# Issuing the five engine programs straight into the main block of a fused attention and GLU kernel

## Chip, cores and metric

One core of one Trainium2 chip. The metric is the device time of one execution in microseconds (us). The *span* is the time from the first to the last instruction record of an execution; it is shorter than the device time. The three sets of experiments ran on three different chips, so times are compared within a set.

## The reference, cut

```python
def _A_ref(x, wqkv, wo):            # sliding window attention: 32 heads of 18, window 256
    ...
def _B_ref(x, w_gate, w_up, w_down):
    g = jnp.einsum("bsd,df->bsf", x, w_gate)
    u = jnp.einsum("bsd,df->bsf", x, w_up)
    h = _sigmoid(g) * u
    return jnp.einsum("bsf,fd->bsd", h, w_down)

x = A_x                              # 2048 x 576, bf16
xn = _layernorm(x, axis=-1)
s = _A_ref(xn, A_wqkv, A_wo)
g = _silu(_B_ref(xn, B_w_gate, B_w_up, B_w_down))   # hidden size 4608
return x + s * g
```

## The kernel before

The kernel builds a graph of operations, orders it with its own scheduler, and then emits one program for each engine. Only the emission matters here. `run_engine` writes an engine's instructions with their semaphore waits. Ahead of SyncE's last operation, which is the last store of the output, it writes a wait for every DMA lane (semaphore) that is not an output lane; after it, a wait for the output lanes.

```python
        def run_engine(e, eng):
            known = {}
            for o in self.prog[e]:
                if e == "SP" and o is self.prog[e][-1]:
                    for i, n in enumerate(lane_cnt):
                        if n > 0 and i not in outs:
                            eng.wait_ge(lanes[i], n)        # housekeeping waits
                # ... the operation's own waits, the operation, its semaphore update ...
            if e == "SP":
                for i in outs:
                    eng.wait_ge(lanes[i], lane_cnt[i])      # the output has landed
                eng.nop()

        with nc.Block() as block:
            @block.tensor
            def _(eng):
                run_engine("PE", eng)
            # ... scalar, vector, gpsimd and sync likewise ...
```

`nc.Block()` gives each engine a block of its own with a branch into it and a branch out of it, and closes with an all-engine barrier: each engine drains and signals, GpSimd gathers the signals and releases the others.

The softmax here doesn't subtract the row's maximum and nothing guards it: scores larger than these inputs give would overflow.

## Time and profile before

| | before |
|---|---|
| device time, median of the first 3 runs | 560.82 us (560.54 to 561.11) |
| span of the profiled run, its device time | 558.90 us, 560.63 us |
| TensorE busy | 553.0 us, 99% of the span |
| last store lands (SyncE's wait ends) to end of the span | 0.437 us |

The prediction below shows the lines. Two habits help. In the source view of a line, each row is one engine's instructions of that line: durations in ns, then the first and the last start in us. A "q" after an engine's name marks its sequencer, which waits, branches and issues and never counts as busy. Where a start or end is quoted to the nanosecond, it is from the trace's records.

### The profile page before, as it was taken

The page shows a single profiled execution, that of the slowest core. Times are in us where ns is not written, and L with a number is a line of the kernel's source. Part 1 is how long each engine was busy: PE and PEld are TensorE (multiplying, and loading weights), DVE is VectorE, ACT ScalarE, POOL GpSimd, SP SyncE. Part 2 cuts the span into 40 slices and gives each one's busy share as a digit, 9 for nine tenths or more (in the row PEclk, how much of TensorE's full clock was granted, in tenths as well). Part 3 has the DMA queues.
Part 4 walks back from the last instruction along what each step waited for, and adds up shares of the span by engine and source line. Part 5 has one row for each costly group of instructions (what it writes and reads, how often), then busy time and mean ns, then how long its engine had stood idle before and what let it go on. Part 6 is the DMA issues. An engine that isn't in the chain of part 4 may idle for free.

```text
span 558.9 us, 19273 instructions
## 1 busy us (share of the span) xinstructions
PE 553.0 (99%) x8342; PEld 339.5 (61%) x8342; DVE 333.6 (60%) x797; ACT 274.3 (49%) x383; POOL 210.8 (38%) x360
## 2 busy tenths in 40 slices
PE   8999999999999999999999999999999999999996
PEld 7454444677755545467886555545688754444786
DVE  5477788687568767574558757357567623333033
ACT  4245654443657655645656464565756342323011
POOL 5564456566245444440667534035373200000000
PEclk9999999999999999999999999999999999999999
DMA  8988997831125534435121264244501035551010
GB/s 224 311 239 191 218 270 221 204 51 45 54 71 155 161 110 144 139 112 95 28 62 44 78 196 115 84 134 130 166 24 47 20 110 154 160 171 48 2 45 23
DMA packets 113468, 67.83 MB, mean 121 GB/s; under 512 B 18620, under 2 KB 111516, under 8 KB 113384
## 3 DMA queue, kind: packets, MB, share of 16 engines
q1 hardware_dynamic: 105960, 60.68, 39.8%
q0 software_dynamic: 7424, 5.92, 4.0%
q8 instruction: 66, 1.08, 0.8%
q14 instruction: 18, 0.15, 0.1%
HBM read 55.15 MB, written 2.36 MB: 103 GB/s over the span
## 4 chain that ended last, share of the span: by engine, by line
PE 98%; DVE 1%; DMA 0%; issue 0%; DVEq 0%
PE ps L121 94%; PE ps L800 3%; DMA x<-in_A_x_dram 0%; DVE small L524 0%; DVE small L526 0%; PE ps L598 0%; DVE xnr L540 0%; DVE s_attn L1061 0%; DVE thf L1066 0%; DVE xnr L544 0%; DVE small L528 0%; DVE small L530 0%; DVE xf L1071 0%; DVEq L1226 0%
## 5 line engine op out<-in xcount | busy, mean ns | idle before, releaser
L121 PE MATMUL ps<-xnT,wgs 64*128 64x512 bf16 (+1 forms) x2400 | 282.5, 368 | 0.1
L750 ACT ACTIVATE expr<-ps 128x1024 bf16<-128x1024 f32 (+4 forms) x160 | 154.9, 969 | 77.8 <-PE ps L121 77.2
L121 PEld LDWEIGHTS ps<-xnT,wgs 64*128 64x128 bf16 x2400 | 113.9, 94 | 114.8 <-DVE hT L948 1.6
L121 PE MATMUL ps<-wd_sb,hT 64*128 64x288 bf16 (+2 forms) x2448 | 156.7, 276 | 0.0
L948 DVE SCALAR_TENSOR_TENSOR hT<-tring,ps 128x512 bf16<-128x512 bf16 x144 | 98.3, 683 | 94.5 <-ACT tring L945 93.4
L945 ACT ACTIVATE tring<-ps 128x512 bf16<-128x512 f32 x144 | 86.1, 598 | 129.7 <-PE ps L121 127.5
L121 PEld LDWEIGHTS ps<-wd_sb,hT 64*128 64x128 bf16 x2448 | 112.4, 94 | 28.6
L278 POOL DMA_DIRECT2D qk<-qd x160 | 82.5, 522 | 119.4 <-PE ps L121 109.5
L763 DVE TENSOR_TENSOR expr<-expr,mask 128x128 bf16<-128x128 bf16 (+2 forms) x240 | 63.6, 298 | 62.0 <-ACT expr L750 61.5
L714 POOL TENSOR_SCALAR kx<-kprev,small 128x256 bf16<-128x256 bf16 x64 | 61.4, 969 | 28.1 <-PE ps L121 27.4
L121 PE MATMUL ps<-qk,kx 64*128 64x320 bf16 (+1 forms) x704 | 59.4, 254 | 0.0
L278 POOL DMA_DIRECT2D oT<-o2T x72 | 36.5, 514 | 58.5 <-DVE o2T L826 49.6
L121 PE MATMUL ps<-xnT,wgr 64*128 64x512 bf16 (+1 forms) x300 | 55.9, 367 | 0.0
L121 PEld LDWEIGHTS ps<-qk,kx 64*128 64x128 bf16 x704 | 31.2, 94 | 21.5 <-ACT expr L750 0.5
L121 PE MATMUL ps<-xnT,wqk 64*128 64x512 bf16 x256 | 32.6, 376 | 0.0
L1051 ACT ACTIVATE thf<-ps 128x576 bf16<-128x576 f32 (+3 forms) x22 | 11.4, 519 | 39.7 <-PE ps L121 39.4
L818 DVE STREAM_TRANSPOSE ot<-ps 128x512 f32<-128x512 f32 x32 | 22.4, 700 | 11.6 <-PE ps L800 11.5
L714 DVE TENSOR_SCALAR kx<-qk,small 128x512 bf16<-128x512 bf16 x64 | 22.4, 378 | 4.7 <-PE ps L121 4.1
L121 PEld LDWEIGHTS ps<-xnT,wgr 64*128 64x128 bf16 x300 | 14.9, 94 | 16.5
L826 DVE STREAM_TRANSPOSE o2T<-o 128x512 bf16<-128x512 bf16 x32 | 22.7, 711 | 1.0
L636 DVE CAST qd<-ps 128x1024 bf16<-128x1024 f32 (+1 forms) x20 | 22.1, 1110 | 1.5 <-PE ps L121 1.5
L696 ACT ACTIVATE v_aug<-ps 64x288 bf16<-64x288 f32 x32 | 13.1, 409 | 17.3 <-PE ps L121 16.8
(71 smaller groups left out, 302.1 us busy)
## 6 DMA issues: line engine op xcount, KB each, us to landing
wgs<-in_B_w_gate_dram SPq DMA_DIRECT2D x72, 256.0 KB, 3.3
wgs<-in_B_w_up_dram SPq DMA_DIRECT2D x72, 256.0 KB, 3.7
wd_sb<-in_B_w_down_dram SPq DMA_DIRECT2D x9, 576.0 KB, 6.3
qk<-qd POOLq DMA_DIRECT2D x100, 36.0 KB, 2.7
wgr<-in_B_w_gate_dram SPq DMA_DIRECT2D x36, 64.0 KB, 2.2
wgr<-in_B_w_up_dram SPq DMA_DIRECT2D x36, 64.0 KB, 2.5
xf<-in_A_x_dram SPq DMA_DIRECT2D x16, 144.0 KB, 2.6
out_dram<-xf SPq DMA_DIRECT2D x15, 144.0 KB, 1.8
```

The source lines that it names most:

```text
L121: res = eng.matmul(outs[i], lhs(ROWS[t], i), rhs(ROWS[t], i), start=start, stop=stop, tile_position=(64 * t, 0))
L278: o = self.op(eng, DMA_ISSUE_NS[eng], lambda e: e.dma_start(dst, src), name, deps, prio, nbytes=nbytes)
L636: return eng.tensor_copy(dst, self.both(h, n))
L696: return eng.activation(dst, src, ACTF.Copy)
L714: return e.tensor_scalar(self.kx[:, sx, pos:pos + n_ // SW, t, :], src.rearrange("p (s k) -> p s k", k=SW), self.half[:, t:t + 1], None, A ...
L750: return eng.activation(self.expr[:, se, :, lo * SW:NT], self.both(h, NT)[:, :, lo * SW:NT], ACTF.Exp, scale=SM_SCALE)
L763: return eng.tensor_tensor(e_, e_, m_, ALU.mult)
L800: res = eng.matmul(outs[i][p0:p0 + VH, cols], self.v_aug[ROWS[i], o:o + VH], self.expr[ROWS[i], se, t, cols], start=n == 0, stop=n == len( ...
L818: return e.transpose(self.ot1[:, p1, :], self.halves(hp, NT)[i])
L826: t2 = op("DVE", dve_ns(NT), lambda e, p2=p2, p3=p3: e.transpose(self.o2T[:, p3, :], self.o2[:, p2, :]), f"ot2:{c}:{pr}:{i}", deps=[on, d3 ...
L945: th = op("ACT", act_ns(NT), lambda e: e.activation(self.tring[:, st, :], bank(h, 0), ACTF.Tanh, scale=0.5), f"th:{c}:{ft}", deps=[pg, dt_ ...
L948: mu = op("DVE", dve_ns(NT), lambda e: e.scalar_tensor_tensor(self.hT[:, ft, :], self.tring[:, st, :], 1.0, bank(h, 1), ALU.add, ALU.mult) ...
```

## The change

The intent is to do without the blocks: no branches, and no barrier at the end, since SyncE already waits for the output itself.

```diff
-        with nc.Block() as block:
-            @block.tensor
-            def _(eng):
-                run_engine("PE", eng)
-  ... (scalar, vector, gpsimd, sync likewise)
+        for e, eng in (("SP", nc.sync), ("POOL", nc.gpsimd), ("DVE", nc.vector), ("ACT", nc.scalar), ("PE", nc.tensor)):
+            run_engine(e, eng)
```

## The prediction

> **What bounds the kernel now.** I read the page's busy table and slices first, then the chain that ended last, then the two ends of the span, because the change touches nothing between them.
>
> ```profile
> span 558.9 us, 19273 instructions
> PE 553.0 (99%) x8342; PEld 339.5 (61%) x8342; DVE 333.6 (60%) x797; ACT 274.3 (49%) x383; POOL 210.8 (38%) x360
> PE   8999999999999999999999999999999999999996
> ...
> PE 98%; DVE 1%; DMA 0%; issue 0%; DVEq 0%
> ```
>
> The reader is to see that TensorE is busy in all slices but the first and the last, and that 98% of the chain is TensorE. Nothing in the middle can shrink unless matmuls go, and none do. A change to the frame round the program can act only in the first microsecond and in what follows the last matmul (the 6 in the last slice).
>
> The end, from the chain cut to 550 to 559 us:
>
> ```profile
> 549.98 4.54 PE ps L121 x170
> ...
> 554.92 0.28 DVE s_attn L1061
> ...
> 555.23 0.41 DVE thf L1066
> ...
> 555.66 0.27 DVE xf L1071
> ```
>
> TensorE ends at about 554.5, and VectorE finishes the last rows at 555.93. The span goes on for another 2.96 us, and that rest is SyncE's. The source views of the lines that SyncE runs last give it:
>
> ```profile
> L1216 SPq EVENT_SEMAPHORE  x31: 28/28/28, 554.9 to 556.8; - x31
> ...
> L1226 SPq EVENT_SEMAPHORE  x1: 28/28/28, 556.8 to 556.8; - x1
> ...
> L278 SPq DMA_DIRECT2D out_dram<-xf x1: 332/332/332, 556.9 to 556.9; - x1
> ...
> L1233 SPq EVENT_SEMAPHORE  x1: 1188/1188/1188, 557.3 to 557.3; - x1
> ```
>
> Columns are duration in ns (min, median, max), then first and last start. SyncE runs down 31 housekeeping waits at about 60 ns each, issues the last store at 556.89, and sits in its wait for that store until 558.458 (the trace's nanosecond record: 557.270 plus 1,188 ns). Only then comes what the change removes, on the line of the framework's block:
>
> ```profile
> L1235 POOLq EVENT_SEMAPHORE  x2: 17/17/17, 558.7 to 558.8; - x2
> L1235 POOLq DRAIN  x1: 10354/10354/10354, 446.2 to 446.2; - x1
> L1235 PEldq DRAIN  x1: 732/732/732, 553.8 to 553.8; - x1
> L1235 ACTq DRAIN  x1: 294/294/294, 554.9 to 554.9; - x1
> L1235 DVEq DRAIN  x1: 311/311/311, 555.7 to 555.7; - x1
> L1235 SPq COMPARE_BRANCH  x1: 41/41/41, 558.5 to 558.5; - x1
> L1235 SPq DRAIN  x1: 13/13/13, 558.7 to 558.7; - x1
> L1235 SPq EVENT_SEMAPHORE  x1: 17/17/17, 558.8 to 558.8; - x1
> L1235 ACTq EVENT_SEMAPHORE  x1: 17/17/17, 558.8 to 558.8; - x1
> L1235 DVEq EVENT_SEMAPHORE  x1: 21/21/21, 558.8 to 558.8; - x1
> L1235 PEldq EVENT_SEMAPHORE  x1: 51/51/51, 558.8 to 558.8; - x1
> ```
>
> The closing barrier is a drain per engine, a gather on POOL, and a release back to all. Four engines arrive early: their long drains (POOL's 10,354 ns) lie beside other work and cost nothing. SyncE arrives last, so only its branch, its drain, the gather and the release stand after the output.
>
> **What the Trainium skill says.** "Perfetto Trace Analysis", section "Sequencer-only Instruction (DRAIN, etc)": for such an instruction the profiler reports only the execution, not the semaphore wait or the propagation after it. The trace agrees: the records of the barrier after SyncE's branch have 13, 17, 17 and 51 ns on the path, while the time from that branch's end (558.537) to the last release record (558.895) is 358 ns; most of it is between records. So I take start-to-start distances, not durations. "VectorE: DVE Perf Modes", section "The DRAIN you can't avoid", puts frame drains at about 12 ns; SyncE's 13 agrees, the others are longer since their engines still had work. "Advanced Engine Details and Errata", section "Control Flow Timing", gives about 51 ns for an unconditional branch; the only branch recorded is SyncE's, 41 ns, followed by 138 ns to the next record. "Runtime: NRT & Kernel Launch", section "The ~15µs preamble/postamble breakdown", has the runtime's own barrier after the kernel, about 1.5 us; the trace holds no record of it, but the profiled execution's time, 560.63, is 1.73 us above its span of 558.90, so something of that size follows or precedes the span.
>
> **The change part by part.** The instruction orders of the two built programs differ only by the entry and exit branches of each engine, and the built program's last block, which the change drops, holds the barrier: four drains with their waits, and POOL's drain with its two semaphore instructions. Every matmul, DMA and wait keeps its place on its engine. The start-up barrier belongs to the framework's preamble, not to the block, and stays.
>
> At the end: after 558.458 the new SyncE program has one more wait (two output lanes, long since satisfied), where the old one has a wait folded into its branch. In the run of 31 waits one takes about 60 ns from end to end, so SyncE should end at 558.458 + 0.060 = 558.518. Before, the last record ends at 558.895. Saving: 0.377 us. It is wholly on the path, because nothing else is running.
>
> The parts of that 0.377: from the wait's end to SyncE's drain 0.217 (558.458 to 558.675), to POOL's gather 0.038 (558.713), to the release instruction 0.077 (558.790), to the latest engine's wake 0.054 (558.844), that record 0.051; sum 0.437, less the 0.060 that the remaining wait costs.
>
> At the start: five entry branches go. But none of them has a record, and SyncE's first DMA starts at 0.798, 66 ns after the start-up barrier released SyncE at 0.732. At the end, between its last wait (556.853) and the DMA (556.893), the gap is 40 ns with no branch at all. So an entry branch can have cost at most 26 ns, less than the exit branch with its 138 ns gap; I think the entries fall through. I count 0.013, half of it. VectorE's first memset begins 131 ns after its release, but the first matmuls it starts are warm-up, and the first real chain begins with the load of x, on SyncE.
>
> In the middle: 0. TensorE's order is unchanged.
>
> Sum inside the span: 0.377 + 0.013 = 0.39 us, so span 558.5 and time 560.82 - 0.39 = 560.43.
>
> Outside the span there are about 1.7 us that no record explains. With the barrier all five engines leave the program within some 60 ns of each other; without it four leave 2.5 us or more before SyncE, so whatever each one does before the runtime's own barrier is done by then. If SyncE is the slowest there too, this gains nothing; if another is, up to 1 us. My estimate, with no measurement behind the odds: 0.08 on average. The predicted time is 560.35.
>
> **The rivals.** One: the barrier was hidden, because the runtime's barrier replaces it and takes the same wait. Then the span shrinks by 0.39 but the time does not move: 560.8. For it: both gather on SyncE, and the output wait is the same. Against: the two stand in series, each with its own round of semaphores. Two: the early departure above frees a larger part of the 1.73 us, giving 559.5 to 560.0. For it: that part is four times larger than the removed barrier. Against: SyncE also has to pass through it, and it leaves last. Three: the code's place in memory moves by the few instructions dropped, so instruction fetches fall elsewhere. A stall on TensorE would add up to microseconds; but the chain now shows 0% "issue", over 8,342 matmuls, so the stream is fed with room to spare, and a straight stream is no harder to fetch than one with branches. I give it 0 to 0.1. Four: an engine that starts tens of nanoseconds earlier shifts the first transfers against each other; the start has slack in x's landing, and it would be worth 0.1 either way.
>
> **Range and chances.** The three runs before spread from 560.54 to 561.11, about 0.3 each way, as large as the effect. From the point 560.35, the second rival and a low draw give 559.8; the first rival with a little noise gives 560.9. Two per cent is 11.2 us, thirty times the barrier and more than everything outside TensorE's busy time (558.9 - 553.0 = 5.9). Faster by that needs something that the trace does not show: 0.01. Slower needs a fetch stall repeated through the program: 0.01.
>
> **What would show it.** Right: no record on the block's line at the end; the last record is SyncE's wait for the outputs, within 0.1 us after the last store lands; a span of 558.5; SyncE's first DMA still at 0.78 to 0.80; TensorE's busy time within 0.3 us of 553.0; time minus span still about 1.7. Wrong at the outside step: time minus span clearly below 1.7 (rival two) or above by 0.4 (rival one). Wrong at the start step: first DMA or first matmul over 50 ns earlier. Wrong in the middle: a new "issue" share on the chain or a longer TensorE.

## The result, and the profile after

The changed kernel took 560.06 us (median of 6 runs, 559.74 to 560.31) against 560.92 us (6 runs, 560.54 to 561.15). The ratio is 0.9984, with a 95% interval of 0.9972 to 0.9997; a ratio is the mean time of one kernel's runs over that of the other's of the same rounds, so not quite the ratio of the medians. That is 0.86 us less, within 2% and inside the range, but nearly twice the saving that was forecast: 0.39 + 0.08 = 0.47 us, from 560.82 to 560.35.

The page of the kernel after, the lines that answer to those of before:

```profile
span 559.0 us, 19262 instructions
PE 552.0 (99%) x8342; PEld 338.4 (61%) x8342; DVE 333.4 (60%) x797; ACT 274.2 (49%) x383; POOL 210.2 (38%) x360
PE   8999999999999999999999999999999999999997
...
PE 98%; DMA 1%; SPq 1%; DVE 0%; issue 0%; DVEq 0%
```

Read alone this puzzles: eleven records fewer, yet the span is no shorter (558.98 against 558.90) while the device time of this very run, 560.31, is lower than the 560.63 of before. Two things lie on top of each other. The first is in the body, the stretch from the first record to the end of VectorE's last row. The chain of waits of the kernel after, cut to the first 12 us (start, length, what):

```profile
4.25 4.02 DMA wgr<-in_B_w_up_dram
8.28 0.09 issue
8.37 0.46 PE ps L121 x10
```

In this profile a weight tile landed late and TensorE waited 0.285 us for it (the record before ends at 8.082, the next starts at 8.367). A second gap of 0.230 us follows at 10.53, which the chain puts to "issue", so no recorded wait explains it. In the profile of before the chain ran over the load of x instead. VectorE finished its last row at 556.390, against 555.932. So the body was 0.46 us longer in this one execution. The busy times in windows, first of before, then of after (window, length, then busy us and count of each engine, clock, DMA), show where it is:

```profile
0.00:12.00 12.00, 10.60 (x278) 9.95 (x280) 6.48 (x31) 5.13 (x9) 5.37 (x16) 1.00 0.79 220
12.00:554.00 542.00, 541.86 (x8059) 329.22 (x8054) 325.45 (x761) 268.69 (x372) 205.40 (x345) 1.00 0.44 120
```

```profile
0.00:12.00 12.00, 9.21 (x263) 8.51 (x265) 6.48 (x31) 5.13 (x9) 5.64 (x16) 1.00 0.79 219
12.00:554.00 542.00, 541.86 (x8055) 329.12 (x8050) 324.86 (x760) 268.53 (x372) 204.59 (x345) 1.00 0.44 120
```

After the first 12 us TensorE is as full as before, to the hundredth (the first engine figure). The difference is all in the opening. (Of the 1.39 us by which TensorE's busy time differs there, 0.87 is idle time in its warm-up before 7.28 us, which delays nothing.) Three profiles of this same program, the changed kernel unaltered, have VectorE's end at 556.390, 556.110 and 555.961, a spread of 0.43, so this part is chance and not the change. The spans of the other runs say so too: in the same rounds they average 559.1 us for before and 558.6 for the changed kernel in the first set of experiments below, 559.3 and 558.7 in the third. The profile of before was a short draw.

The second thing is the end. The source views of SyncE's last lines in the kernel after:

```profile
L1216 SPq EVENT_SEMAPHORE  x31: 27/28/28, 555.4 to 557.2; - x31
...
L1232 SPq EVENT_SEMAPHORE  x1: 17/17/17, 558.9 to 558.9; - x1
...
L1233 SPq EVENT_SEMAPHORE  x1: 28/28/28, 559.0 to 559.0; - x1
```

No record of a barrier follows. The wait for the last store ends at 558.919, one more wait at 558.978, and the span is over: 0.059 us after the landing instead of 0.437. From VectorE's end to the end of the span it is 2.588 us instead of 2.963. That is 0.38 us, and the runs show another gain of about that size that is in no record: time minus span was 1.73 us in the profiled run of before and 1.22 to 1.34 (mean 1.29) in the six runs of after. The experiments are about that second half.

### The profile page after: what moved, and what is told of

Its sections match the earlier page's. It is cut to its first block, busy times and chain, and to the rows that moved or that the text cites. A ratio compares the mean times of both kernels' runs of the same rounds, so it can differ in the third digit from the quotient of the medians.

```text
span 559.0 us, 19262 instructions
## 1 busy us (share of the span) xinstructions
PE 552.0 (99%) x8342; PEld 338.4 (61%) x8342; DVE 333.4 (60%) x797; ACT 274.2 (49%) x383; POOL 210.2 (38%) x360
## 4 chain that ended last, share of the span: by engine, by line
PE 98%; DMA 1%; SPq 1%; DVE 0%; issue 0%; DVEq 0%
PE ps L121 94%; PE ps L800 3%; DMA wgr<-in_B_w_up_dram 1%; SPq L278 1%; DVE s_attn L1061 0%; DVE thf L1066 0%; PE ps L598 0%; DVE xf L1071 0%; DVEq L1226 0%
```

## The experiments

Time minus span is a sharp measure here, because the body's chance (spans of before differ by up to 1.1 us from run to run) is in both and drops out. The record has the spans of unprofiled runs to 0.1 us, so a single difference is uncertain by 0.05. Theory A: after its last record each engine still has a way out of the program, these ways run side by side, one is slower than SyncE's, and an engine that leaves early gets it done while SyncE still waits. Rival B: the barrier's instructions lengthen what follows, whenever the engines leave. Rival C: chance. In the tables, "tail" is from the landing of the last store (the end of SyncE's wait for it) to the end of the span in the profiled run; times are means of the runs.

### First set: the same kernel, all engines late, the barrier alone

`e1_again`: the changed kernel, no edit.

> The changed kernel once more, unaltered, as the base of this set. Time minus span was 1.73 us in the profiled run of the kernel before and 1.22 to 1.34 us in six runs of the changed one. If that drop of about 0.43 us belongs to the change, it is here again (1.2 to 1.4) and the time is 0.7 to 0.9 us below before. If it was chance, time minus span is somewhere near 1.7 and the gain is only the 0.38 us inside the span. The profiled start: if the late weight transfer (TensorE waits 0.3 to 0.5 us at 7.9 us) is chance it need not be here; if it comes from the change it is.

`e2_all_wait`: every engine ends with SyncE's wait.

```diff
-            if e == "SP":
+            if e in ('SP', 'PE', 'ACT', 'DVE', 'POOL'):
                 for i in outs:
                     eng.wait_ge(lanes[i], lane_cnt[i])
                 eng.nop()
```

> The changed kernel, but all five engines end with the wait for the output stores that SyncE alone has; no barrier, no blocks. Theory A (engines that leave early do their part of the end outside the program while SyncE still waits, and one of them is slower at it than SyncE): time minus span goes back to about 1.7, the span stays within 0.15 of the changed kernel's, the time is 0.3 to 0.5 us above it. Theory B (the barrier's own instructions lengthen what follows, it does not matter when engines leave): time minus span stays at 1.2 to 1.4 and the time is within 0.15 us of the changed kernel.

`e3_barrier`: the barrier without the blocks.

```diff
             run_engine(e, eng)
+        nc.all_engine_barrier()
```

> The changed kernel with the framework's all-engine barrier put back at the end of the main block, without the blocks and their branches. If the barrier is the whole cost: time within 0.15 us of before, span 0.25 to 0.4 above the changed kernel's, time minus span 1.7. If branches and blocks cost something: 0.1 to 0.4 us below before. The exit branch of SyncE had 41 ns and 138 ns after it, so about 0.1 to 0.15 us of the 0.38 should be missing here if that branch is the cause of that gap.

| same rounds | runs | time | median | time minus span | tail |
|---|---|---|---|---|---|
| before | 9 | 560.88 | 560.74 | 1.79 | 0.437 (first profile) |
| e1_again | 5 | 559.86 | 559.86 | 1.26 | 0.060 |
| e2_all_wait | 5 | 560.81 | 560.82 | 1.81 | 0.157 |
| e3_barrier | 5 | 560.67 | 560.77 | 1.75 | 0.324 |

The unaltered kernel reproduces its gain (ratio 0.9981, interval 0.9969 to 0.9994) and its low time minus span, so C falls for that half. It also opens over the load of x, with no late weight tile, as before did.

The second run decides between A and B. It has no barrier, no branch and no drain, and time minus span is back at 1.81 (1.78 to 1.84 over five runs). That its time, 560.81 us, is all the way back at that of before is partly luck: of the 0.95 us above e1_again, 0.55 is time minus span and 0.10 the longer tail; the other 0.3 is a longer body, and both its span and its time are further above e1_again than theory A expected (0.15 and 0.5 at most). All five engines leave together, as the source view of the closing wait in this kernel shows:

```profile
L1233 SPq EVENT_SEMAPHORE  x1: 28/28/28, 558.9 to 558.9; - x1
L1233 ACTq EVENT_SEMAPHORE  x1: 38/38/38, 558.9 to 558.9; - x1
L1233 POOLq EVENT_SEMAPHORE  x1: 43/43/43, 558.9 to 558.9; - x1
L1233 DVEq EVENT_SEMAPHORE  x1: 50/50/50, 558.9 to 558.9; - x1
L1233 PEldq EVENT_SEMAPHORE  x1: 51/51/51, 559.0 to 559.0; - x1
```

It is when engines leave that costs 0.5 us, not what they leave through. B falls.

The barrier alone is as slow as before within the noise (560.67 against 560.88, ratio 0.9995, interval 0.9981 to 1.0009). Its tail divides the 0.377 us of the records: 0.324 less the 0.060 of the changed kernel is 0.264 for the barrier itself, and 0.437 less 0.324 is 0.113 for the block's exit branch on SyncE. The drain on the barrier's line of this kernel starts at 558.954, 40 ns after the record before it, where it took 138 ns after the branch:

```profile
L1237 SPq DRAIN  x1: 13/13/13, 559.0 to 559.0; - x1
L1237 SPq EVENT_SEMAPHORE  x1: 17/17/17, 559.1 to 559.1; - x1
```

### Second set: one late engine at a time

`e5_pe`, `e5_pool`, `e5_act`, `e5_dve`: the edit of e2_all_wait, with SyncE and one other engine in the list.

```diff
-            if e == "SP":
+            if e in ('SP', 'POOL'):      # or 'PE', 'ACT', 'DVE'
```

> The changed kernel, with TensorE too ending in the wait for the output stores; the other three leave early. If one slow engine makes the 0.52 us (time minus span 1.81 with all five late, 1.26 to 1.29 with SyncE alone late) and it is TensorE, whose semaphore records are the longest (51 ns against 17): time minus span 1.7 to 1.85, time about 560.5 to 560.8. If the cost is a chain that every late engine lengthens a little: about 1.4. If TensorE is not in it: 1.2 to 1.3.

> The same with GpSimd as the second late engine. One slow engine and it is GpSimd: time minus span 1.7 to 1.85. A chain that every late engine lengthens: about 1.4. Not in it: 1.2 to 1.3. GpSimd is the rival to TensorE for the slow one, since its drain in the kernel before ran 10 us.

> The same with ScalarE as the second late engine. One slow engine theory: I expect 1.2 to 1.3, since nothing in the records sets ScalarE apart from SyncE (17 ns records, same order of release). Chain theory: about 1.4.

> The same with VectorE as the second late engine. One slow engine theory: 1.2 to 1.35 (its records are 21 ns against 17, so it may be a little slower than SyncE). Chain theory: about 1.4.

| late besides SyncE | runs | time | time minus span | tail |
|---|---|---|---|---|
| VectorE | 4 | 560.38 | 1.31 (1.29 to 1.33) | 0.112 |
| ScalarE | 4 | 560.27 | 1.42 (1.42 to 1.43) | 0.080 |
| TensorE | 4 | 560.43 | 1.51 (1.45 to 1.57) | 0.156 |
| GpSimd | 4 | 560.83 | 1.83 (1.80 to 1.90) | 0.095 |
| before, same rounds | 7 | 561.09 | 1.76 | |

The times alone would not tell the first three apart; time minus span does. The slow engine is GpSimd: late alone beside SyncE, it brings back all of the 1.8. The closing wait in that kernel:

```profile
L1233 SPq EVENT_SEMAPHORE  x1: 28/28/28, 558.9 to 558.9; - x1
L1233 POOLq EVENT_SEMAPHORE  x1: 43/43/43, 558.9 to 558.9; - x1
```

I had TensorE as the first guess and named GpSimd as its rival; TensorE's 1.51 is in none of the three ranges that I gave: it has a slow way out too, but not the slowest. ScalarE is slower than SyncE by some 0.1, which I did not expect; its 1.42 is the chain theory's figure. VectorE can't be told from SyncE (1.25 to 1.32 over six sets of runs in which SyncE alone is late, all of them from the other two sets of experiments; this one has none). The chain rival falls in its simple form: the excesses over SyncE's 1.29 add up to 0.02 + 0.13 + 0.22 + 0.54 = 0.91, while all five late cost 0.52. The largest decides. Another form of it stands untested: a hand-over in a fixed order, in which a late engine holds up only those behind it, would give the same figures as ways out that run side by side.

In before, TensorE's record ends the span, and GpSimd's last record is 0.088 us earlier (558.807 of 558.895). From that record it is 1.79 + 0.09 = 1.88 to the end of the time. The same sum gives 1.87 in e2_all_wait and 1.84 in e3_barrier, next to 1.83 where GpSimd is the late one. So in all four the end of the time fits GpSimd's way out.

### Third set: controls, and a better kernel

`f2_control`: as many added wait instructions on the four engines, but on counts reached at VectorE's end.

```diff
                 eng.nop()
+            else:
+                for i in outs:
+                    if lane_cnt[i] > 16:
+                        eng.wait_ge(lanes[i], lane_cnt[i] - 16)
+                eng.wait_ge(self.sem["DVE"], cnt["DVE"])
+                eng.nop()
```

> Control for the runs with a second late engine: all four other engines end with two added wait instructions, as there, but on counts that are reached at VectorE's end, some 2.3 us before SyncE leaves. If lateness costs: time minus span 1.25 to 1.32 as in the changed kernel. If the added instructions themselves do (their place in memory, a fetch, another way out of the program): about 1.8 as with all five late.

`f3_no_pool`: a barrier over four engines.

```diff
             run_engine(e, eng)
+        nc.multi_engine_barrier([mybir.EngineType.SP, mybir.EngineType.Activation, mybir.EngineType.PE, mybir.EngineType.DVE])
```

> The changed kernel with the framework's barrier at the end over four engines, GpSimd left out, so that it leaves 100 us early; ScalarE leads it. If each engine has its own way out after its last record and the slowest decides (GpSimd about 1.85 us, TensorE about 1.51, ScalarE 1.42, VectorE and SyncE 1.3): TensorE is last now, time minus span 1.45 to 1.57, not 1.75; the span's tail after the last store's landing stays near the 0.32 of the five-engine barrier; time 0.2 to 0.35 us below before. If any barrier costs what the old one did: 1.75 and the time of the five-engine barrier.

`f4_after`: the changed kernel, no edit, as the base of these rounds.

> The changed kernel unaltered, in the same rounds as the three above, to compare with: time minus span 1.24 to 1.34, time 0.8 to 1.0 us below before.

| same rounds | runs | time | median | time minus span | tail |
|---|---|---|---|---|---|
| before | 9 | 561.03 | 560.98 | 1.75 | |
| f4_after | 5 | 560.02 | 559.95 | 1.32 | 0.060 |
| f2_control | 4 | 560.06 | 559.91 | 1.29 | 0.058 |
| f3_no_pool | 4 | 560.72 | 560.71 | 1.57 | 0.304 |

The added waits cost nothing when they end 2.4 us before SyncE leaves (GpSimd's last record is at 556.113, the span's end at 558.575). So lateness is the cause, and not the added instructions. With GpSimd left out, the barrier keeps its tail (0.304 against 0.324) but time minus span falls from 1.75 to 1.57, near TensorE's 1.51: the next largest decides now.

### Taking the housekeeping waits off the end

While reading the end I saw that SyncE issues the last store 0.96 us after VectorE made its data, because it is still running down 31 waits at 61 ns each. They are on lanes whose transfers are over long before.

`e4_early` (first set) moves them ahead of the third last operation, where SyncE idles:

```diff
-                if e == "SP" and o is self.prog[e][-1]:
+                if e == "SP" and o is self.prog[e][-3]:
```

> The changed kernel with SyncE's 31 housekeeping waits moved from before the last store to before the third last, where SyncE idles for 9 us. The last store should then be issued within 0.1 us of VectorE's end instead of 0.96 us after it: 0.85 us off the end, time about 559.2 (0.8 to 0.9 below the changed kernel), time minus span unchanged at 1.2 to 1.4. If the landing of the last store then meets the one before it, less: 0.4.

`f1_best` (third set) also changes the order of the closing waits:

```diff
-                for i in outs:
+                for i in sorted(outs, key=lambda i: i != self.prog[e][-1].lane):
```

The framework emits those three waits as two instructions in the reverse order, so the key puts the last store's lane first in order to have it waited for last.

> The changed kernel with the early housekeeping waits and with the output lanes waited for in such an order that the last store's lane comes last, so that no further wait follows its landing. From the earlier set, whose last store came 28 ns after VectorE's end: the end of the span should now be the record of the wait on the last store, 0.06 us less than the early waits alone; from VectorE's end to the span's end about 1.60 us (1.66 there, 2.60 in the changed kernel). Time minus span as for SyncE leaving last alone, 1.25 to 1.32. Time 0.6 to 1.0 us below the changed kernel's of the same rounds.

The waits of e4_early, in the source view, and its last two stores, in the timeline; then the same timeline line of the kernel after (start, length from the first issue to the end of the second, count):

```profile
L1216 SPq EVENT_SEMAPHORE  x31: 27/28/28, 541.6 to 544.2; - x31
...
554.95 1.77 SPq L278 DMA_DIRECT2D out_dram<-xf  x2
```

```profile
554.98 2.70 SPq L278 DMA_DIRECT2D out_dram<-xf  x2
```

The pair of stores takes 0.93 us less. The last one is issued 28 ns after VectorE's end instead of 957. In f1_best nothing follows the wait for the landing, which is now on the other line:

```profile
L1233 SPq EVENT_SEMAPHORE  x1: 28/28/28, 557.8 to 557.8; - x1
```

| | time | same-round base | VectorE's end to the span's end | time minus span |
|---|---|---|---|---|
| e4_early | 559.25 (median 559.28) | e1_again 559.86 | 1.664 (base 2.599) | 1.29 |
| f1_best | 559.19 (median 559.17) | f4_after 560.02 | 1.611 (base 2.601) | 1.25 |

The end shrank as expected, by 0.94 and 0.99 us. The times fell by 0.61 and 0.83, the first less than the 0.8 to 0.9 that I expected. In the profiled runs the bodies of these two were longer than their bases' (VectorE's end 556.364 against 556.110, and 556.178 against 555.961), and both opened over a late weight tile, as did other runs with no such edit. I take that for the same chance as in the first profile of after, but five runs each don't exclude that the early waits cost some of it. f1_best is the fastest kernel: 559.17 us against 560.98 for before in the same rounds, ratio 0.9968 (0.9955 to 0.9980).

## Why the prediction was right or wrong

- *What bounds the kernel, and 0 in the middle*: right. TensorE is busy for 541.86 us of 542 between 12 and 554 us in both. But the sign that I gave for it, TensorE's busy time within 0.3 us of 553.0, was too strict. It was 552.0 in the first profile of the changed kernel and 553.2 and 551.9 in its copies; the difference is in the opening.
- *The end inside the span, 0.377 us*: right (the predicted span of 558.5 was not: it left out the body's chance, and the profiled run of after has 558.98). The tail went from 0.437 to 0.059, a saving of 0.378, on the path as argued. The split was right too: the 138 ns gap after SyncE's branch belonged to the branch (0.113 for the whole exit branch, net of the wait folded into it), the rest to the barrier. One reading is too wide: of the profiler's records of sequencer instructions the prediction says that they leave out the wait for semaphores and that the trace agrees. That holds for the barrier's records, but SyncE's record of 1,188 ns, in its own list, is a wait that lasts until 22 ns after the last store landed (558.436). In the changed kernel the wait for the same store is a record of 17 ns that starts after the landing.
- *The start, 0.013 us*: right to count nearly nothing. SyncE's first DMA starts at 0.798 before and at 0.795, 0.797 and 0.799 in three profiles of after. Entry branches cost nothing that can be seen.
- *Outside the span, 0.08 us on average*: this is the step that failed. It was mis-sized more than fivefold, and it is the main reason that 0.86 was measured where 0.47 was said. The mechanism, an engine slower than SyncE on the way out, was named, but as a rival with low odds, and the engine was not. The runs show 0.43 to 0.53 us (time minus span 1.75 to 1.79 before against 1.26 to 1.32 in same-round copies), and the engine is GpSimd. The prediction's own sign for it, time minus span clearly below 1.7, came true. The argument that I put against it, that SyncE has to pass the same part and leaves last, missed that SyncE's own way out is half a microsecond shorter than GpSimd's. Also, the five engines leave before over 88 ns, not some 60, since GpSimd's last record ends first. That the measured time fell inside the range owes something to the range's width: the rival's own figure was 559.5 to 560.0.
- *Rival one, a barrier that was hidden*: wrong; both halves came off the time. Its argument that both barriers gather on SyncE does not fit the record: the removed one gathers on GpSimd (L1235). *Rival three, fetches*: no sign that the change brought any; f2_control, with the code moved again, is at the same time as its base. But "fed with room to spare" is not shown: in six of the fourteen profiles TensorE stands still for 0.14 to 0.25 us at about 10.5 us, each time at the same matmul and with no recorded wait. It comes and goes in one and the same program (in the first profile of after, not in e1_again or f4_after). A late fetch of instructions would look like that; no run tests it.
- *What is not explained*: 0.38 and 0.43 to 0.53 make 0.81 to 0.91 us, and the three pairs of means differ by 0.87, 1.02 and 1.01. The remaining 0.05 to 0.2 us is in the span and less than the body's chance. No record shows what an engine does between its last record and the end of the time; that this is the frame's work round the program is my reading. The Trainium skill, "Runtime: NRT & Kernel Launch", section "The ~15µs preamble/postamble breakdown", has a closing barrier of about 1.5 us there, and after it two more steps of about 1.5 and 2 us. Time minus span, 1.25 to 1.83 depending on which engine leaves last, is near the first alone and well under their sum; no run shows which of these steps it holds.

## What to carry to other kernels

Compare time minus span as well as the span: a change to how a program ends can gain as much after the last record as before it. Let only the engine that must wait for the output be last, SyncE if possible, and let the others, GpSimd above all, run out of their programs early. A closing barrier does the opposite. Keep bookkeeping out of the stretch between the last result and the last store: moving it away shortened the end by 0.94 us here.

## What the runs showed of the hardware that was not expected

- Time minus span depends on the engine that leaves last: SyncE 1.25 to 1.32 us, VectorE no more than 1.31, ScalarE 1.42, TensorE 1.51 to 1.57, GpSimd 1.83. Where several leave late, the largest figure decides and not the sum. The whole figures may hold time before the first record; only their differences are shown to belong to the end.
- One more housekeeping wait on SyncE costs 61 ns from start to start although its record is 28 ns long and its transfer is over; 31 of them stood between the last result and its store.
- The opening alone moves the body of the same program by 0.43 us between three profiles, at a granted clock of 0.999 to 1.000. The spans of 25 runs of before in the three sets differ by up to 1.1 us (558.7 to 559.8); where the runs without a trace lose it is not seen.

## What the Trainium skill lacked or had wrong

- "Runtime: NRT & Kernel Launch", "The ~15µs preamble/postamble breakdown", gives one figure for the closing barrier of the runtime, about 1.5 us. It lacks that the time outside the span depends on which engine leaves last: 1.25 to 1.32 us for SyncE alone, 1.83 where GpSimd is as late.
- No page that I read says what the framework's closing barrier costs: 0.26 us in the records and 0.43 to 0.53 us after them, plus 0.11 us for SyncE's exit branch.
- "Advanced Engine Details and Errata", "Control Flow Timing", has about 51 ns for an unconditional branch and about 108 ns for compare-and-branch. The prediction compared with the first; the one recorded at the end is named COMPARE_BRANCH. It has 41 ns, and 138 ns more pass before the next record, where 40 ns pass without a branch; entry branches into the next block left neither a record nor a measurable gap (from the release of SyncE to its first DMA it is 66 ns with them, 61 to 66 without).
